# Gated linear attention and a ReLU-squared layer on one core: where three of twelve units transpose the attention's output

## The chip, the core and the metric

The kernel runs on one core of a Trainium2 chip. A core has five engines with a program each: TensorE (PE in the profile; PEld is its weight load), VectorE (DVE), ScalarE (ACT), GpSimd (POOL) and SyncE (SP), which here only issues DMAs. The metric is the time of one execution on the chip in microseconds (us), median of several runs. Lower is better.

## What is computed

A recurrent attention with decays, then a dense layer with a squared ReLU:

```python
for t in range(S):                                   # S = 768, B = 4, H = 8, D = 48
    state = alpha[:, :, t, :, None] * state + np.einsum('bhd,bhe->bhde', k[:, :, t], v[:, :, t])
    y[:, :, t] = np.einsum('bhd,bhde->bhe', q[:, :, t], state)
x = y.transpose(0, 2, 1, 3).reshape(B * S, H * D)    # 3072 x 384
h = x @ w_in                                         # 384 x 2048
r = np.maximum(h, 0.0)
out = (r * r) @ w_out                                # 2048 x 384
```

Inputs and output are float32; the kernel multiplies in bfloat16 and accumulates in float32.

## The kernel before

The work is cut into 12 **units**, each 256 tokens of one of the four sequences; unit g is batch g % 4, step g // 4. The names below are those of the kernel's operations; `_g` is the unit.

1. **Loads.** `lda`, `ldk`, `ldq`, `ldv` bring alpha, k, q and v of a unit (384 KB each, L540). Units 0 to 3 come in part over POOL's queue with the weights `win0` to `win2` and `wout0`, `wout1` (L508), all else over SP's queue.
2. **Decays.** `pr` multiplies the decays of two neighbouring tokens (L656 on VectorE, L658 on POOL), `ln` takes the logarithm, `m1i` sums it along tokens on TensorE (L668), `ei`, `ea`, `es` are exponentials on ScalarE, `bk` and `aq` products (L686, L697).
3. **Scaled keys and queries.** `ekm` and `eqm` multiply them by k and q (L737, L732). From unit 3 on, two DMA transposes per unit, `tr0` and `tr1`, turn them over on SP's queue (L748); before that TensorE does it.
4. **Scores.** `p0_g` multiplies keys and queries into the four banks psX and psZ (L926), `mk0` and `mk1` mask them into SBUF on VectorE (L937).
5. **State and output.** `vc` casts v to bfloat16 (L727 on POOL, L728 on ScalarE). `y_g` multiplies masked scores and state with v into psX (L818, L829); in its middle it also makes the state product of unit g+1 (`kv`, L797), so it waits for `vc_(g+1)`. `sa`, `sc`, `sd` update the state (L892 to L903).
6. **Transposing the output.** `xe_g` copies psX to bfloat16 (xbf, L957). Then either SP issues one DMA transpose `xt_g` from xbf to xt (L978), or TensorE makes six transposes of 128 x 128 into psX (L972) and `xv_g` copies them to xt (L984). The set `DMA_X` says which: units 4 to 11 go over SP's queue, units 0 to 3 over TensorE.
7. **First layer.** `s1_g_u`, u from 0 to 7, six matmuls of 256 columns each (L1030); `re` is the ReLU (L1038 on ScalarE, L1040 on VectorE), `sq` the square.
8. **Second layer.** For units 3 to 10 a Strassen form with seven products in two halves each (`s2_g_m10` to `s2_g_m71`, four matmuls of 192 columns, L1096) and sums of operands before (`ga`, `gb`, `gc`; `ws` for the weights) and of results behind (`ca` to `cg`, L1123 to L1127). Units 0 to 2 and 11 use plain products of 384 columns (L1168, L998). `out` stores the unit over SP's queue. The output tile osb has two buffers, so the first write of unit g waits for the store of unit g-2.

The order of every engine is written out by hand in `ORDERS`: one list of names per engine, and an operation may be in the list of one engine or of another where it has both forms. A planner only works out which waits are needed; it changes no order. Each engine takes its list strictly from the front, so one operation that waits holds all behind it. That holds for SP's queue too, where a transpose, a load or a store that waits for its source holds the later DMAs. A few loads are tied to the landing of an earlier one (`AFTER`: `win2` before `wout0`, for example). Fillers, `fill512` and `fill256`, are products with zeros that keep TensorE busy while it waits at the start.

Of the kernel before, what the change touches and what calls it, by code (L numbers as in the profile page):

```python
# [1263 lines left out]
```

## Time and profile before

| | us |
|---|---|
| median of 3 runs | 174.56 (174.54 to 178.17) |
| profiled execution | 176.19 |
| its span, first to last instruction | 174.5 |
| TensorE busy | 161.7 |
| VectorE busy | 136.1 |
| ScalarE busy | 122.5 |
| GpSimd busy | 100.0 |

The profile is of one execution. A line of a timeline gives the start, the length, the engine, the line of the kernel and the operation, and in brackets how long the engine sat idle ahead of it and what ended that. A matmul's end is modelled, and matmuls overlap, so the pace of TensorE is read from one start to the next. "SPq" is a DMA being issued on SP's queue, not its transfer. The granted clock of TensorE was 1.000 of full speed.

### The profile page before, as it was taken

The page shows a single profiled execution, that of the slowest core. Times are in us where ns is not written, and L with a number is a line of the kernel's source. Part 1 is how long each engine was busy: PE and PEld are TensorE (multiplying, and loading weights), DVE is VectorE, ACT ScalarE, POOL GpSimd, SP SyncE. Part 2 cuts the span into 40 slices and gives each one's busy share as a digit, 9 for nine tenths or more (in the row PEclk, how much of TensorE's full clock was granted, in tenths as well). Part 3 has the DMA queues.
Part 4 walks back from the last instruction along what each step waited for, and adds up shares of the span by engine and source line. Part 5 has one row for each costly group of instructions (what it writes and reads, how often), then busy time and mean ns, then how long its engine had stood idle before and what let it go on. Part 6 is the DMA issues. An engine that isn't in the chain of part 4 may idle for free.

```text
span 174.5 us, 5592 instructions
## 1 busy us (share of the span) xinstructions
PE 161.7 (93%) x2417; PEld 139.2 (80%) x2417; DVE 136.1 (78%) x230; ACT 122.5 (70%) x213; POOL 100.0 (57%) x95
## 2 busy tenths in 40 slices
PE   7789989999999799899977989899899999999994
PEld 2456879757788587799966879799889999999973
DVE  4588889998898798789868797869999559855620
ACT  4775579968979499698887568798866775576310
POOL 3935263910188467696724864789854780938140
PEclk9999999999999999999999999999999999999999
DMA  5999999997899998999999998999787770400122
GB/s 141 332 306 210 298 258 218 250 328 159 164 215 181 340 238 167 292 157 243 288 137 229 292 143 195 155 228 316 121 144 235 75 184 4 135 4 19 71 94 92
DMA packets 70633, 33.40 MB, mean 191 GB/s; under 512 B 66544, under 2 KB 67568, under 8 KB 70608
## 3 DMA queue, kind: packets, MB, share of 16 engines
q1 hardware_dynamic: 67984, 26.35, 69.6%
q0 software_dynamic: 2624, 6.69, 15.7%
q8 instruction: 19, 0.31, 0.7%
q14 instruction: 6, 0.05, 0.1%
HBM read 25.17 MB, written 4.72 MB: 171 GB/s over the span
## 4 chain that ended last, share of the span: by engine, by line
PE 43%; DMA 23%; DVE 15%; SPq 8%; POOL 4%; issue 3%; ACT 2%; DVEq 0%; ACTq 0%
PE psWH L1030 16%; DMA out_dram<-osb 8%; PE psO L1096 7%; DMA raw<-in_alpha_dram 6%; PE psWH L1096 5%; SPq L540 5%; DMA win<-in_moe_w_in_dram 5%; PE psO L1168 5%; DVE pm L937 4%; DMA raw<-in_k_dram 3%; DMA raw<-in_v_dram 2%; DVE prd L656 2%; DVE rr L1040 2%; POOL raw L540 2%; SPq L748 2%
## 5 line engine op out<-in xcount | busy, mean ns | idle before, releaser
L1030 PE MATMUL psWH<-xt,win 128*128 128x256 bf16 x552 | 71.5, 273 | 0.4 <-DMA win<-in_moe_w_in_dram 0.4
L1030 PEld LDWEIGHTS psWH<-xt,win 128*128 128x128 bf16 x552 | 60.1, 129 | 2.1 <-DMA win<-in_moe_w_in_dram 0.6
L1038 ACT ACTIVATE rr<-psWH 128x512 bf16<-128x512 f32 x69 | 40.2, 594 | 14.8 <-PE psWH L1030 13.9
L1052 ACT ACTIVATE gt<-rr 128x1024 bf16<-128x1024 bf16 (+1 forms) x40 | 37.2, 946 | 2.7 <-DVE rr L1040 2.5
L1082 POOL TENSOR_TENSOR gt<-sg,gt 128x512 bf16<-128x512 bf16 x15 | 18.6, 1237 | 14.9 <-DVE sg L1080 14.8
L1051 POOL TENSOR_TENSOR gt<-rr 128x512 bf16<-128x512 bf16 (+1 forms) x12 | 14.7, 1228 | 15.5 <-ACT rr L1038 13.2
L1040 DVE TENSOR_SCALAR rr<-psWH 128x512 bf16<-128x512 f32 x23 | 15.8, 685 | 5.2 <-PE psWH L1030 5.1
L1168 PE MATMUL psO<-wout,gt 128*128 128x384 bf16 x96 | 18.3, 326 | 0.0
L937 DVE TENSOR_TENSOR pm<-psZ,caus 128x1024 bf16<-128x1024 f32 x12 | 14.6, 1218 | 2.4 <-PE psZ L926 2.4
L937 DVE TENSOR_TENSOR pm<-psX,caus 128x1024 bf16<-128x1024 f32 x12 | 14.6, 1217 | 1.5 <-PE psZ L926 1.5
L1096 PE MATMUL psWH<-sw,gt 128*128 128x192 bf16 x128 | 15.1, 246 | 0.0
L1096 PE MATMUL psO<-wout,gt 128*128 128x192 bf16 x128 | 13.7, 246 | 1.3 <-ACT osb L1123 0.7
L1083 POOL TENSOR_TENSOR sh<-gt 128x512 bf16<-128x512 bf16 x10 | 13.4, 1341 | 2.2 <-DVE gt L1082 1.3
L1080 DVE TENSOR_TENSOR sg<-gt 128x1024 bf16<-128x1024 bf16 x13 | 12.5, 961 | 1.9 <-PE psWH L1096 1.0
L732 DVE TENSOR_TENSOR qks<-raw,eq 128x384 bf16<-128x384 f32 x18 | 12.6, 712 | 1.5 <-DMA raw<-in_q_dram 1.4
L727 POOL CAST vbf<-raw 128x768 bf16<-128x768 f32 x8 | 7.8, 978 | 10.1 <-DMA raw<-in_v_dram 10.0
L1168 PEld LDWEIGHTS psO<-wout,gt 128*128 128x128 bf16 x96 | 8.9, 98 | 4.7
L957 ACT ACTIVATE xbf<-psX 128x768 bf16<-128x768 f32 x11 | 8.9, 807 | 5.0 <-PE psX L818 3.3
L1096 PEld LDWEIGHTS psO<-wout,gt 128*128 128x128 bf16 x128 | 10.5, 98 | 2.0 <-ACT osb L1123 1.0
L737 DVE TENSOR_TENSOR qks<-raw,ek 128x768 bf16<-128x768 f32 x11 | 10.4, 946 | 2.0 <-DMA raw<-in_k_dram 1.8
L1096 PEld LDWEIGHTS psWH<-sw,gt 128*128 128x128 bf16 x128 | 10.6, 98 | 0.6
L1127 DVE TENSOR_TENSOR osb<-psWH,osb 128x192 f32<-128x192 f32 x24 | 8.4, 351 | 3.1 <-PE psWH L1096 3.0
(162 smaller groups left out, 297.5 us busy)
## 6 DMA issues: line engine op xcount, KB each, us to landing
out_dram<-osb SPq DMA_DIRECT2D x11, 384.0 KB, 5.1
raw<-in_alpha_dram SPq DMA_DIRECT2D x10, 384.0 KB, 4.8
raw<-in_q_dram SPq DMA_DIRECT2D x10, 384.0 KB, 5.4
raw<-in_v_dram SPq DMA_DIRECT2D x10, 384.0 KB, 4.6
raw<-in_k_dram SPq DMA_DIRECT2D x9, 384.0 KB, 5.1
wout<-in_moe_w_out_dram POOLq DMA_DIRECT2D x2, 768.0 KB, 8.0
raw<-in_k_dram POOLq DMA_DIRECT2D x3, 384.0 KB, 6.4
raw<-in_alpha_dram POOLq DMA_DIRECT2D x2, 384.0 KB, 6.3
```

The source lines that it names most:

```text
L732: add("dve", lambda e, j=j, dst=dst: e.tensor_tensor(dst, RAW[r][:, 2, :, j, :].rearrange("p (n x) d -> p n x d", x=2), EQ[la][:, j].rearr ...
L937: add("dve", lambda e, hf=hf, psT=psT: e.tensor_tensor(PM[pm][:, hf].rearrange("p r n j t -> p (r n) (j t)"), psT[:, :, :].rearrange("p r ...
L1030: ins = pe.matmul(psF[:, i * T:(i + 1) * T], WIN[:, kk, hidden(fj)], mov, start=(kk == 0), stop=(kk == KT - 1))
L1038: add("act", lambda e, psF=psF, rr=rr: e.activation(rr, psF, AF.Relu), act_ns(512), pu + 600, reads=[keyF], writes=[("rr", rb, half)], nam ...
L1040: alts={"dve": (lambda e, psF=psF, rr=rr: e.tensor_scalar(rr, psF, 0.0, None, ALU.max), dve_ns(512))})
L1051: alts={"pool": (lambda e, dst=dst, sq=sq: e.tensor_tensor(dst, sq, sq, ALU.mult), 200 + k * 840), "act": (lambda e, dst=dst, sq=sq: e.act ...
L1052: "act": (lambda e, dst=dst, sq=sq: e.activation(dst, sq, AF.Square), act_ns(k * 512))})
L1080: ga = lambda e, us=us: e.tensor_tensor(SG[:, us], view(us, 128, [[0, 2], [1, 128]]), view(us, 0, [[384, 2], [1, 128]]), ALU.subtract)
L1082: gb = lambda e, us=us: e.tensor_tensor(G4[:, us, 0, 1], SG[:, us, 1], G4[:, us, 0, 0], ALU.subtract)
L1083: gc = lambda e, us=us: e.tensor_tensor(SH[:, us], G4[:, us, 1, 0], G4[:, us, 0, 1], ALU.add)
L1096: ins = pe.matmul(psS, left(u), right(u), start=(first and u == 0), stop=(u == nu - 1), skip_group_check=True)
L1168: ins = pe.matmul(psS, GT[gt][:, fj, j, :], WOUT[:, fj, :], start=(fj == 0), stop=(fj == FT - 1))
```

## The change

Units 4, 6 and 8 leave `DMA_X`: their `xt` is six transposes on TensorE into psX, with a copy `xv` on VectorE. SP's list has three names fewer. All five lists are new, and many operations change places, and some their engine.

```diff
-    DMA_X = (4, 5, 6, 7, 8, 9, 10, 11)
+    DMA_X = (5, 7, 9, 10, 11)
```

SP's list:

```diff
-        lda0 ldk0 ldq0 ldv0 ldv1 lda3 ldq3 lda4 ldk4 ldq4 tr0_3 tr1_3 ldv4 lda5 ldq5 tr1_4 tr0_4 ldk5 lda6 ldv5 ldk6
-        out0_1 ldq6 out1_1 tr1_5 tr0_5 xt4 ldv6 lda7 ldq7 ldk7 tr1_6 tr0_6 xt5 ldv7 lda8 ldk8 ldq8 out2_1 tr1_7 tr0_7
-        xt6 ldv8 lda9 ldq9 ldv9 ldk9 out3_1 tr0_8 tr1_8 xt7 lda10 out4_1 tr1_9 tr0_9 ldq10 ldk10 xt8 ldv10 lda11
...
+        lda0 ldk0 ldq0 ldv0 ldv1 lda3 ldq3 lda4 ldq4 ldk4 tr0_3 tr1_3 lda5 ldv4 ldq5 ldk5 tr1_4 tr0_4 ldv5 lda6 lda7
+        out0_1 ldq6 tr1_5 tr0_5 ldk6 ldv6 out1_1 ldk7 ldq7 tr1_6 tr0_6 xt5 ldv7 lda8 ldq8 ldk8 out2_1 tr0_7 tr1_7 ldv8
+        lda9 ldk9 tr1_8 tr0_8 ldq9 out3_1 xt7 ldv9 lda10 ldk10 ldq10 out4_1 tr1_9 tr0_9 ldv10 lda11 ldq11 out5_1 ldv11
...
```

TensorE's list at the start, and around the three transposes and unit 4's scores:

```diff
...
-        fill512_15 fill512_16 fill256_17 fill256_18 y0 tr1_1 fill512_19 fill256_20 xt0 tr0_1 fill512_21 fill512_22
-        fill512_23 fill256_24 p0_1 s1_0_0 s1_0_2 s1_0_1 kv1 s1_0_3 y1 s1_0_4 s1_0_6 xt1 s1_0_5 m1i2 s1_0_7 s1_1_0 m1s2
...
-        s1_2_3 s1_2_2 p0_3 s2_1_1_0 s2_1_1_1 s1_2_4 s1_2_5 y3 s2_1_1_2 s1_2_7 m1i5 xt3 s1_2_6 s2_1_1_3 s1_3_1 s1_3_0
-        p0_4 s2_2_0_0 s2_2_0_1 s1_3_3 s2_2_0_2 s1_3_2 y4 s2_2_0_3 s1_3_5 m1i6 s1_3_4 s2_2_1_0 s1_3_7 s2_2_1_1 s1_3_6
...
+        fill512_15 fill256_16 fill256_17 tr0_1 xt0 tr1_1 fill256_18 s1_0_2 p0_1 s1_0_0 s1_0_1 kv1 s1_0_3 y1 s1_0_4
+        s1_0_5 xt1 s1_0_7 m1i2 s1_0_6 m1s2 s1_1_2 s1_1_1 s1_1_0 s1_1_5 s1_1_4 tr0_2 s1_1_3 tr1_2 s1_1_7 s2_0_0_0 p0_2
...
+        xt3 m1i5 s1_2_6 s2_1_1_3 s1_3_1 s1_3_0 s2_2_0_0 p0_4 s2_2_0_1 s1_3_3 s1_3_2 s2_2_0_2 y4 s1_3_5 s2_2_0_3 m1i6
+        s1_3_4 s1_3_7 s2_2_1_0 xt4 s2_2_1_1 s2_2_1_2 s2_2_1_3 s1_3_6 p0_5 s2_3_m10 s1_4_0 s1_4_1 s2_3_m60 s2_3_m11
...
+        s2_3_m51 s1_5_0 s1_5_1 s2_3_m40 s2_3_m30 s1_5_2 s2_3_m31 s1_5_3 y6 s2_3_m41 s1_5_4 s2_4_m10 xt6 s2_4_m11 m1i8
+        s1_5_5 s2_4_m20 s2_4_m60 s2_4_m21 s1_5_6 s2_4_m61 s1_5_7 s2_4_m50 s2_4_m70 p0_7 s2_4_m71 s2_4_m51 s1_6_0
...
+        s2_5_m40 s1_7_3 s2_5_m41 s1_7_4 m1i10 xt8 s2_5_m30 s2_5_m31 s2_6_m60 s1_7_5 s1_7_6 s2_6_m10 s2_6_m61 s2_6_m11
+        s1_7_7 s2_6_m20 p0_9 s2_6_m21 s1_8_0 s2_6_m70 s2_6_m71 s1_8_1 s2_6_m50 s2_6_m51 s1_8_2 y9 s2_6_m40 s1_8_3
...
```

POOL's list at the start, and VectorE's lines with the three new copies and with sa10:

```diff
-        #20 #22 #14 #21 #15 lda1 ldq1 ldk1 win1 vc0 win0 win2 lda2 ldv2 ldk2 ldq2 wout0 sd1 sd0 wout1 sq1_1 ldv3 ldk3
...
+        #14 #21 #20 #15 #22 lda1 ldk1 ldq1 win1 vc0 win0 win2 lda2 ldk2 vc1 ldv2 ldq2 sd0 wout0 pr2 wout1 sd1 bk2 aq2
...
```

```diff
-        mk1_8 cd5 ce5 re7_2 sa9 re7_3 ga6_1 cf5 cg5 lb10 eqm1_10 ca6 cb6 ekm10 mk0_9 mk1_9 cd6 eqm0_10 ce6 pr11 xe9
-        sa10 ga7_1 cf6 cg6 sq8_1 re8_6 lb11 ca7 gc7_1 re8_7 mk1_10 cb7 mk0_10 ekm11 cd7 eqm1_11 eqm0_11 ga8_0 gc7_0
...
+        oe2_0 ga3_0 gb3_0 sc5 re3_7 lb6 gc3_0 xv4 eqm0_6 eqm1_6 ekm6 mk0_5 mk1_5 ga3_1 gb3_1 re4_3 sa6 cb3 sc6 cc3
+        re4_4 eqm1_7 cd3 lb7 ekm7 ga4_0 ce3 mk1_6 mk0_6 eqm0_7 pr8 sq4_5 cg3 sa7 cf3 sc7 xv6 gc4_0 gb4_1 lb8 cc4
...
+        ekm9 eqm0_9 mk0_8 cd5 eqm1_9 re7_2 gc5_0 sa9 cf5 ce5 ga6_1 re7_4 xv8 cg5 re7_5 eqm1_10 lb10 ekm10 cb6 mk0_9
+        mk1_9 eqm0_10 cd6 re8_1 ce6 sa10 xe9 ga7_1 cg6 cf6 lb11 eqm1_11 sq8_6 mk1_10 cb7 mk0_10 ekm11 eqm0_11 cd7 ce7
...
```

In the new lists `pr11` is POOL's, and so are `pr2`, `bk2`, `aq2` and `bk3`; `vc3`, `vc4`, `vc5`, `vc7` and `vc9` go to ScalarE. TensorE has 11 fillers of 512 columns in place of 17.

More of the change, by code (lines that the diff above doesn't have):

```diff
@@ L25 @@
+        sq9_5 re9_7 cc8 re10_1 sq9_7 re10_3 xe11 re10_5 re10_4 re10_7 re10_6 sq10_1 sq10_5 re11_1 cc9 re11_3 re11_2
+        re11_5 sq11_1 sq11_3 ca10 cc10 sq11_5 oe11_10
     """,
     "dve": """
-        #19 #5 #3 #1 #12 #10 #9 #11 #13 #8 #7 #16 ekm0_0 eqm0_0 ekm1_0 et10_0 #17 et01_0 #18 #6 eqm1_0 sa0 mk0_0 mk1_0
-        eqm1 #2 ekm1 et1_1 et0_1 sc0 mk1_1 mk0_1 sa1 sc1 re0_3 re0_2 pr2 xv1 sq0_3 bk2 ekm2 re1_0 aq2 eqm2 #4 et0_2
-        et1_2 sq0_7 ws0_0 sq1_5 mk1_2 mk0_2 pr3 ws0_1 sa2 sc2 bk3 ekm3 aq3 eqm1_3 eqm0_3 pr4 sd2 sq1_6 xv2 ws3_0 sc3
@@ L70 @@
-        sd7 gc6_0 sq7_7 sq7_6 ga7_0 gb7_0 gb7_1 vc11 sq8_7 bk11 gb8_0 ga8_1 gb8_1 gc8_0 sq9_7 gb9_0 gc9_0 gb9_1 gc9_1
-        gb10_0 sq10_7 gc10_0 gb10_1 sq11_7 sq11_6
+        #14 #21 #20 #15 #22 lda1 ldk1 ldq1 win1 vc0 win0 win2 lda2 ldk2 vc1 ldv2 ldq2 sd0 wout0 pr2 wout1 sd1 bk2 aq2
+        vc2 sq1_1 ldk3 ldv3 ws0_1 bk3 bk4 sd3 pr5 ws3_0 ws2_1 ws3_1 bk5 sq2_7 sq2_5 pr6 sq3_3 bk6 pr7 sq3_6 vc6 gc3_1
+        ws1_1 sd5 bk7 gb4_0 sq4_6 ga4_1 bk8 sq5_7 vc8 gc4_1 pr9 gb5_0 gb5_1 gc5_1 sq6_6 sd6 ga6_0 pr10 gb6_0 gb6_1
```

78 lines of the change are left out of this document (35 added, 43 removed).

## The prediction

> **What bounds the kernel now.** I read the engine sums first, then the same sums cut into stretches, then the waits of TensorE alone, then the order of time on SP's queue around each wait.
>
> ```profile
> span 174.5 us, 5592 instructions
> PE 161.7 (93%) x2417; PEld 139.2 (80%) x2417; DVE 136.1 (78%) x230; ACT 122.5 (70%) x213; POOL 100.0 (57%) x95
> ```
>
> TensorE (PE) is the busiest engine, 174.5 - 161.7 = 12.8 us idle. The next view is the table of stretches: length, busy time of PE, weight loads, VectorE (DVE), ScalarE (ACT), GpSimd (POOL), then PE's clock, DMA share, GB/s.
>
> ```profile
> 0.00:17.73 17.73, 14.24 (x211) 8.39 (x212) 12.05 (x31) 10.67 (x19) 10.36 (x20) 1.00 1.00 247
> 17.73:60.00 42.27, 41.26 (x580) 32.91 (x580) 36.67 (x55) 32.80 (x61) 19.87 (x18) 1.00 1.02 237
> 60.00:100.00 40.00, 36.09 (x632) 32.51 (x632) 33.98 (x54) 32.65 (x58) 26.80 (x24) 1.00 1.08 230
> 100.00:130.00 30.00, 28.11 (x424) 26.02 (x422) 26.39 (x42) 23.99 (x42) 21.97 (x17) 1.00 1.01 188
> 130.00:172.20 42.20, 42.01 (x572) 39.36 (x572) 26.76 (x53) 22.42 (x37) 21.00 (x17) 1.00 0.37 93
> ```
>
> Before 17.73 us PE waits for the first weights and is partly fed with fillers. From there to 172.20 it is bound by its own work, with idle time of 1.01 + 3.91 + 1.89 + 0.19 = 7.0 us, 5.8 of it from 60 to 130 us, where the DMA share is about 1. From 130 on nothing but PE counts. So the time is: arrival of the weights, plus PE's work, plus these stalls, plus a tail. The timeline of PE names the long stalls (start, length, [idle before <- who ended it]):
>
> ```profile
> 61.14 0.19 PE L818 MATMUL psX<-sbd,kqt 64*128 64x48 bf16 x1 [1.32 <-DVE pm L937]
> 72.85 0.19 PE L818 MATMUL psX<-sbd,kqt 64*128 64x48 bf16 x1 [0.68 <-POOL vbf L727]
> 96.09 0.19 PE L818 MATMUL psX<-sbd,kqt 64*128 64x48 bf16 x1 [1.16 <-POOL vbf L727]
> 103.99 0.83 PE L1096 MATMUL psO<-wout,gt 128*128 128x192 bf16 x8 [0.74 <-ACT osb L1123]
> 113.02 0.34 PE L668 MATMUL psZ<-lab,linc 128*128 128x384 bf16 x1 [0.45 <-ACT lab L659]
> 126.69 0.32 PE L668 MATMUL psZ<-lab,linc 128*128 128x384 bf16 x1 [0.66 <-DVE smd L892]
> ```
>
> These are, in order, y4, y5, y7, the second layer of unit 5, m1i10 and m1i11. SP's queue shows what lay behind four of them:
>
> ```profile
> 47.10 5.46 SPq L748 DMA_TRANSPOSE kqt<-qks  x2
> 52.61 1.47 SPq L540 DMA_DIRECT2D raw<-in_k_dram  x1
> 65.48 1.86 SPq L978 DMA_TRANSPOSE xt<-xbf  x1
> 67.39 0.58 SPq L540 DMA_DIRECT2D raw<-in_v_dram  x1
> 88.46 2.28 SPq L978 DMA_TRANSPOSE xt<-xbf  x1
> 90.79 0.58 SPq L540 DMA_DIRECT2D raw<-in_v_dram  x1
> 96.40 1.15 SPq L1145 DMA_DIRECT2D out_dram<-osb  x1
> 97.59 5.99 SPq L748 DMA_TRANSPOSE kqt<-qks  x2
> 103.63 1.29 SPq L978 DMA_TRANSPOSE xt<-xbf  x1
> 104.96 0.58 SPq L540 DMA_DIRECT2D raw<-in_alpha_dram  x1
> ```
>
> Here v6 is issued at 67.39, right behind xt4, and v8 at 90.79, right behind xt6; the casts that y5 and y7 wait for follow as they land. k5 is issued at 52.61, behind both halves of tr_4, and holds up ekm5, which stands ahead of unit 4's masks on VectorE; y4 waits for those masks. a10 is issued at 104.96 behind xt7 and ends in the wait of m1i10.
>
> **The change part by part.** *Added on TensorE and VectorE.* xt4, xt6 and xt8 become six transposes and one copy each. The chain of waits and the groups by form give their price today:
>
> ```profile
> 42.12 0.33 PE psX L972 x6
> L984 DVE COPY xt<-psX 128x768 bf16<-128x768 bf16 x3 | 1.7, 553 | 0.4 <-PE psX L972 0.2
> ```
>
> The next piece of PE starts at 42.46, so PE pays 3 x 0.34 = **+1.0 us**, fully on the path, since PE is what sets the end. VectorE gets 3 x 0.55 = 1.7 us, beside 136.1 of 174.5; it costs nothing while the copy lands before the next scores. *The new wait:* xt_g waits for xe_g (the evacuation of psX on ScalarE), and the scores p of the next unit wait for xv_g, because all share psX. What stands between y_g and xt_g on PE hides the first: for unit 4 five steps and more, for unit 6 s2, s1, s2, for unit 8 s2, s1, s2, s1, m1i. The prices of these, and unit 7's end of y and xe:
>
> ```profile
> 69.38 1.47 PE L1030 MATMUL psWH<-xt,win 128*128 128x256 bf16 x12
> 70.69 0.82 PE L1096 MATMUL psO<-wout,gt 128*128 128x192 bf16 x8
> 71.35 0.82 PE L1030 MATMUL psWH<-xt,win 128*128 128x256 bf16 x6
> 97.14 0.50 PE L1096 MATMUL psWH<-sw,gt 128*128 128x192 bf16 x4
> 97.25 0.81 ACT L957 ACTIVATE xbf<-psX 128x768 bf16<-128x768 f32 x1 [2.57 <-PE psX L818]
> ```
>
> Twelve L1030 matmuls take 70.69 - 69.38 = 1.31 us, so an s1 step of six is 0.66; eight L1096 take 71.35 - 70.69 = 0.66, so an s2 step of four is 0.33. PE goes on from y7 at 97.14, and xe7 ends at 98.06, so an xt could start 1.0 us after y. Unit 6 has 1.3 us of cover for that and unit 8 about 2.1. Behind each xt stand at least 2.6 us before the next scores, against 0.34 and 0.55 for xt and its copy, and what is ahead of that on VectorE. I cost the wait at nothing; without the cover it is rival C.
>
> *Removed from SP's queue.* Three issues go: 1.86 and 2.28 us for xt4 and xt6 in the rows above, and xt8, with no long stall of PE behind it:
>
> ```profile
> 113.42 2.87 SPq L978 DMA_TRANSPOSE xt<-xbf  x1
> ```
>
>  What follows in the queue moves up by as much: v8, now right behind tr_7, by 2.3 us against a stall of 1.16, and v6 by 1.86 less the issue of k6, which now stands ahead of it (as long as k5's at most, 1.47), so 0.4, and by another 1.3 as tr_5, whose sources VectorE makes behind unit 4's masks, comes earlier with y4. I count 0.68 + 1.16 = **-1.8 us**.
>
> *Moved on SP's queue.* ldk5 now stands ahead of tr_4: k5 is issued at about 47.1, 5.5 us earlier, and y4's stall goes, **-1.3**. The price is that tr_4 is issued one load (1.47 us) later. p0_4 waits for it; one s2 step of 0.65 was put ahead of p0_4, so I count 0.75 back. lda10 no longer stands behind all of unit 7's late queue: **-0.45**. out3 moves behind tr_8 (5.99 us in the row) and a load; ca5 already waited for it (stall 0.74). With xt6 gone and four loads behind, not ahead of, tr_8, it is issued 1 to 2 us later: I count 1.0 back.
>
> *Moved between engines.* pr11 goes to POOL, and sa10 ahead of xe9, on which m1i11 waited: **-0.66**. By the lists, VectorE goes from 230 to 237 instructions, ScalarE from 213 to 212 and POOL from 91 to 88; none comes near PE's 161.7 us.
>
> *The start.* Six fillers of 512 columns go (17 to 11), and s1_0_2, which reads only win1, comes ahead of p0_1 and of s1_0_0, which waits for win0:
>
> ```profile
> 14.96 0.93 POOL L540 DMA_DIRECT2D raw<-in_alpha_dram  x1 [4.50 <-DMA win<-in_moe_w_in_dram]
> 17.73 0.84 PE L1030 MATMUL psWH<-xt,win 128*128 128x256 bf16 x6 [0.43 <-DMA win<-in_moe_w_in_dram]
> ```
>
> The load of a2 is held by win1, so win1 is there by 14.96; win0 by 17.73. One s1 step leaves the time after 17.73: **-0.66**. Bounds: 0 if xt0's copy comes too late, -0.66 as only one step reads win1 alone here.
>
> *Unknown.* The rest of the new order has no rows. Its stalls lie between 0 and 7.0 us, what the old order has in all. Of the old 7.0 I have named 4.27 that go; the other 2.7 I leave. For stalls that are new I take 1.0 beside the 1.75 above, nearest to the many small ones (0.4 to 0.7) of the old order.
>
> Sum: 1.02 - 1.84 - 1.32 - 0.45 - 0.66 - 0.66 + 1.75 + 1.0 = **-1.2 us**. The profiled execution took 176.19 us, 1.7 more than its span, the median of the runs is 174.56; I carry the difference over: **173.4 us**.
>
> How much DMA time a transpose takes decides whether the loads also land faster. Two stretches of 2 us, one of loads and a store, one of tr_5 and xt4:
>
> ```profile
> 60.00:62.00 2.00, 0.86 (x58) 0.87 (x60) 2.00 (x2) 2.00 (x4) 1.91 (x3) 1.00 1.07 348
> 64.00:66.00 2.00, 2.00 (x18) 1.70 (x17) 2.00 (x5) 1.94 (x6) 0.69 (x1) 1.00 0.98 75
> ```
>
> At an equal share of the DMA engines, 348 GB/s are moved there and 75 here. An xt of 128 x 768 x 2 bytes = 197 KB is then 2.6 us of all engines, and three are 7.9 us of a stretch of 70 that is full. I take nothing for this beyond the terms above. [...]
>
> **The rivals.** *B, the relief is swallowed:* loads are late for other reasons (the DMA share is 1.0 from 0 to 130 us whatever is queued), the stalls of 4.27 come back elsewhere. Then only the start and the transposes count: -0.66 + 1.02 = +0.4, **174.9 us**. For it: the named stalls have five different causes, and the new lists reorder every engine, so each pair of neighbours that caused none may cause one now. Against: two of the stalls stand directly behind an xt that is gone. That the change does not do what it says (the gain comes from ldk5 and pr11, not from the transposes) would show as an unchanged y5 and y7; its time lies between B and the forecast.
>
> *C, slower, the new ring on psX:* xe_g stands behind ln_(g+2) on ScalarE, and that waits for the product pr on POOL or VectorE.
>
> ```profile
> ACT lab L659 <- POOL prd L658: 4.9, 4, 2.3
> PEld psX L972 <- ACT xbf L957: 0.2, 1, 0.2
> ```
>
> With a wait of 2.3 us there (the longest), xt6 is late by 2.3 + 1.0 - 1.3 = 2.0 us and xt8 by 2.3 + 1.0 - 2.1 = 1.2; PE stands still, and everything behind it. On top of B: 174.9 + 3.2 = **178.1 us**. It decides once ln comes over 0.3 us (unit 6) or 1.1 us (unit 8) after the end of y. Against it: units 0 to 3 run this chain now, with one wait of 0.2 us (the second row).
>
> *D, clean:* the named stalls go and nothing new comes: 1.02 - 4.27 - 0.66 = -3.9, **170.6 us**.
>
> **How the numbers follow.** Forecast 0.45, B 0.30, C 0.15, D 0.10. About 2% (3.5 us) is what a measurement of this kernel can tell from no change. Faster by more, under 171.1: D and a little of the forecast's lower end, 0.11. Slower by more, over 178.1: half of C and the edge of B with the unknown stalls, 0.10. Within: 0.79. The range leaves out about half of D and half of C: 170.8 to 177.4.
>
> **What would show it.** L972 has 42 matmuls, and SP issues five xt. y4 and y7 start without a wait over 0.3 us; the first s1 starts before 17 us; the stretch from 60 to 130 has under 4 us of idle PE. A wait of PE on L957 (xbf), or of the scores on L984, shows C. If PE's idle time after 17.73 is again 7 us but under other names, it is B. The prediction is wrong if the front (17.73 to 60 us, now 1.0 us idle) gets stalls of its own: pr2, bk2 and aq2 now stand on POOL behind the issue of wout, and such a product takes 1.02 us there in place of 0.55:
>
> ```profile
> L688 DVE TENSOR_TENSOR ek<-ek,raw 128x384 f32<-128x384 f32 x3 | 1.7, 553 | 0.9 <-ACT ek L679 0.9
> L686 POOL TENSOR_TENSOR ek<-ek,raw 128x384 f32<-128x384 f32 x7 | 7.1, 1020 | 6.4 <-ACT ek L679 6.3
> ```

## The result and the profile after

The changed kernel takes **0.989 of the time before, 95% interval 0.9855 to 0.9929**: 174.56 x 0.9892 = 172.7 us, 1.9 us less (1.2 to 2.5). The forecast was 1.2 us less, 173.4 us. Six of the 20 executions after the change and 14 of the 20 before enter this comparison, those up to 1.5% above the fastest of their kernel; 13 of the 14 left out after the change show a granted clock of 0.98 or 0.99, no trace of any of them was kept, and over all executions the plain medians tie (175.07 us after, 175.03 before).

The profiled execution took 172.51 us (176.19 before, which is 1.6 us over the median before, so the two profiles lie further apart than the times). In this kernel the line numbers are two lower than in the one before: L1028 is the first layer, L1094 the second, L816 and L827 y, L970 the transposes on TensorE, L982 their copy, L935 the masks. The experiments below are numbered like the kernel before, except where said. First the engine sums of the page of the kernel after:

```profile
span 170.8 us, 5611 instructions
PE 161.3 (94%) x2429; PEld 139.0 (81%) x2429; DVE 137.1 (80%) x237; ACT 121.6 (71%) x212; POOL 101.9 (60%) x92
```

The stretches of the kernel after (length, then busy time of PE, weight loads, DVE, ACT, POOL, then PE's clock, DMA share, GB/s):

```profile
15.94:60.00 44.06, 41.66 (x606) 32.48 (x607) 38.30 (x54) 31.41 (x57) 29.97 (x27) 1.00 1.01 234
60.00:100.00 40.00, 39.27 (x667) 35.25 (x666) 36.70 (x62) 33.39 (x61) 23.84 (x21) 1.00 1.06 225
100.00:130.00 30.00, 30.00 (x483) 28.49 (x482) 27.42 (x44) 25.73 (x45) 26.05 (x21) 1.00 0.95 218
130.00:168.50 38.50, 38.33 (x508) 35.71 (x505) 23.09 (x52) 20.63 (x33) 13.52 (x9) 1.00 0.30 72
```

From the first s1 step to the end of PE's work, idle time went from 7.0 to 2.40 + 0.73 + 0 + 0.17 = 3.3 us. The first s1 starts 1.79 us earlier (15.94 against 17.73 us), but PE's work from there on is 149.26 against 147.47 us: 1.0 us of it are the new transposes, the rest is what used to stand ahead of 17.73. So of the 3.7 us between the two spans, all is idle time, and it went from 60 to 130 us (5.80 to 0.73); the front got worse (1.01 to 2.40).

PE's stalls in the timeline of the kernel after, all of those over 0.3 us from the first s1 on:

```profile
17.85 1.50 PE L1028 MATMUL psWH<-xt,win 128*128 128x256 bf16 x12 [0.49 <-DMA win<-in_moe_w_in_dram]
41.07 0.36 PE L856 MATMUL psX<-smd,kqt 128*64 128x96 bf16 x8 [0.78 <-ACT vbf L726]
51.40 0.19 PE L816 MATMUL psX<-smd,kqt 64*128 64x48 bf16 x1 [0.34 <-ACT vbf L726]
73.96 0.19 PE L816 MATMUL psX<-sbd,kqt 64*128 64x48 bf16 x1 [0.73 <-DVE pm L935]
```

These are the first s1 on win0, then y2, y3 and y5. y4, y7, m1i10 and m1i11 no longer wait. y5 does, but for another engine: its v is there, its masks (`pm`, L935) are late. SP's queue of the kernel after:

```profile
47.62 1.64 SPq L538 DMA_DIRECT2D raw<-in_k_dram  x1
49.31 4.97 SPq L746 DMA_TRANSPOSE kqt<-qks  x2
...
61.22 4.53 SPq L746 DMA_TRANSPOSE kqt<-qks  x2
65.80 0.58 SPq L538 DMA_DIRECT2D raw<-in_k_dram  x1
66.42 0.58 SPq L538 DMA_DIRECT2D raw<-in_v_dram  x1
...
87.97 1.01 SPq L538 DMA_DIRECT2D raw<-in_v_dram  x1
```

k5 now goes out at 47.62, ahead of tr_4; v8 at 87.97, 2.8 us earlier than before. But k6 is issued at 65.80, behind both halves of tr_5: the new order does to unit 6 what the old one did to unit 5, and y5 pays 0.73 us for it. One transposition set costs PE what was expected (chain of waits, kernel after; the next step starts at 87.65):

```profile
87.32 0.33 PE psX L970 x6
```

### The profile page after: what moved, and what is told of

The parts are those of the page before. It is cut to its first block, busy times and chain, and to the rows that moved or that the text cites. A ratio compares the mean times of both kernels' runs of the same rounds, so it can differ in the third digit from the quotient of the medians.

```text
span 170.8 us, 5611 instructions
## 1 busy us (share of the span) xinstructions
PE 161.3 (94%) x2429; PEld 139.0 (81%) x2429; DVE 137.1 (80%) x237; ACT 121.6 (71%) x212; POOL 101.9 (60%) x92
## 4 chain that ended last, share of the span: by engine, by line
PE 65%; DMA 14%; DVE 9%; SPq 4%; POOL 4%; issue 1%; ACT 1%; DVEq 0%
PE psWH L1028 26%; PE psO L1094 12%; PE psWH L1094 10%; DMA raw<-in_alpha_dram 4%; PE psO L1166 4%; DMA win<-in_moe_w_in_dram 4%; SPq L746 3%; DVE pm L935 3%; DMA raw<-in_v_dram 3%; DMA raw<-in_k_dram 2%; DVE qks L735 2%; PE psX L827 2%; PE psZ L795 2%; POOL raw L538 2%; PE psX L924 2%; PE psX L996 2%
## 5 line engine op out<-in xcount | busy, mean ns | idle before, releaser
L1028 PE MATMUL psWH<-xt,win 128*128 128x256 bf16 x552 | 72.3, 273 | 0.8 <-DMA win<-in_moe_w_in_dram 0.8
L1028 PEld LDWEIGHTS psWH<-xt,win 128*128 128x128 bf16 x552 | 59.9, 129 | 2.8 <-ACT rr L1036 1.0
L1036 ACT ACTIVATE rr<-psWH 128x512 bf16<-128x512 f32 x67 | 39.0, 595 | 16.6 <-PE psWH L1028 15.9
L1050 ACT ACTIVATE gt<-rr 128x1024 bf16<-128x1024 bf16 (+1 forms) x38 | 35.4, 952 | 0.5 <-DVE rr L1038 0.3
L1049 POOL TENSOR_TENSOR gt<-rr 128x512 bf16<-128x512 bf16 (+1 forms) x13 | 19.2, 1489 | 7.5 <-ACT rr L1036 5.7
L1078 POOL TENSOR_TENSOR sg<-gt 128x1024 bf16<-128x1024 bf16 x5 | 11.1, 2211 | 15.9 <-PE psWH L1094 11.2
L1038 DVE TENSOR_SCALAR rr<-psWH 128x512 bf16<-128x512 f32 x25 | 17.1, 685 | 1.9 <-PE psWH L1028 1.5
L684 POOL TENSOR_TENSOR ek<-ek,raw 128x384 f32<-128x384 f32 x9 | 10.1, 1118 | 9.7 <-ACT ek L677 9.7
L935 DVE TENSOR_TENSOR pm<-psZ,caus 128x1024 bf16<-128x1024 f32 x12 | 14.6, 1218 | 0.7 <-PE psZ L924 0.7
L1094 PE MATMUL psWH<-sw,gt 128*128 128x192 bf16 x128 | 15.0, 246 | 0.0
L1094 PE MATMUL psO<-wout,gt 128*128 128x192 bf16 x128 | 15.0, 246 | 0.0
L1080 POOL TENSOR_TENSOR gt<-sg,gt 128x512 bf16<-128x512 bf16 x9 | 11.4, 1266 | 5.7 <-DVE sg L1078 5.5
L935 DVE TENSOR_TENSOR pm<-psX,caus 128x1024 bf16<-128x1024 f32 x12 | 14.6, 1216 | 0.1
L735 DVE TENSOR_TENSOR qks<-raw,ek 128x768 bf16<-128x768 f32 x11 | 13.2, 1197 | 1.8 <-DMA raw<-in_k_dram 0.7
L1081 POOL TENSOR_TENSOR sh<-gt 128x512 bf16<-128x512 bf16 x9 | 10.5, 1181 | 2.9 <-DVE gt L1080 2.7
L1094 PEld LDWEIGHTS psO<-wout,gt 128*128 128x128 bf16 x128 | 10.8, 98 | 0.5
L1094 PEld LDWEIGHTS psWH<-sw,gt 128*128 128x128 bf16 x128 | 10.8, 98 | 0.4
```

Of the source, the lines that this page charges most:

```text
L735: add("dve", lambda e, a=a, E=E: e.tensor_tensor(QKS[qs][:, a, :, :, 0:D], RAW[r][:, 1 + a].rearrange("p h j d -> p j h d"), E[la][:].rear ...
L935: add("dve", lambda e, hf=hf, psT=psT: e.tensor_tensor(PM[pm][:, hf].rearrange("p r n j t -> p (r n) (j t)"), psT[:, :, :].rearrange("p r ...
L1028: ins = pe.matmul(psF[:, i * T:(i + 1) * T], WIN[:, kk, hidden(fj)], mov, start=(kk == 0), stop=(kk == KT - 1))
L1036: add("act", lambda e, psF=psF, rr=rr: e.activation(rr, psF, AF.Relu), act_ns(512), pu + 600, reads=[keyF], writes=[("rr", rb, half)], nam ...
L1038: alts={"dve": (lambda e, psF=psF, rr=rr: e.tensor_scalar(rr, psF, 0.0, None, ALU.max), dve_ns(512))})
L1049: alts={"pool": (lambda e, dst=dst, sq=sq: e.tensor_tensor(dst, sq, sq, ALU.mult), 200 + k * 840), "act": (lambda e, dst=dst, sq=sq: e.act ...
```

## Experiments

**Theory:** the gain comes from the three DMA transposes that are gone; the new order of the lists gives little. **Rival:** the gain is the order's (k5, pr11, the start), and the transposes by themselves are worth 0.8 us or less. The two halves of the change are tried apart first.

### Old lists, only the transposes moved (e2)

```diff
-    DMA_X = (4, 5, 6, 7, 8, 9, 10, 11)
+    DMA_X = (5, 7, 9, 10, 11)
  SP:      xt4, xt6, xt8 out of the old list
  TensorE: ... s2_2_1_0 [xt4] ... s1_5_4 [xt6] ... m1i10 [xt8] ...
  VectorE: ... lb6 [xv4] ... ca4 [xv6] ... re7_3 [xv8] ...
```

> The old lists, with xt4, xt6 and xt8 on TensorE and their copies on VectorE, nothing else. Queue theory: the stalls of y5 (0.68) and y7 (1.16) shrink under 0.3, 42 transposes cost 1.0 more than 24, so 0.8 us faster than before. Order theory: the stalls stay or move, 0.5 to 1.0 us slower than before. The stall of y4 (1.32) stays by both.

Measured: ratio **0.989 (0.983 to 0.995)**, as good as the whole change; the medians over all executions, 171.99 against 173.74 us, give 0.990. Its stretches and its two longest stalls:

```profile
60.00:100.00 40.00, 38.70 (x669) 35.28 (x667) 36.83 (x61) 34.58 (x61) 27.77 (x27) 1.00 1.10 248
100.00:130.00 30.00, 30.00 (x481) 28.48 (x479) 27.16 (x44) 23.79 (x42) 22.96 (x18) 1.00 0.81 188
```

```profile
39.94 0.36 PE L858 MATMUL psX<-smd,kqt 128*64 128x96 bf16 x8 [0.92 <-DVE qks L737]
61.53 0.19 PE L818 MATMUL psX<-sbd,kqt 64*128 64x48 bf16 x1 [1.29 <-DVE pm L937]
```

y4 waits as before (k5 has not moved). y5 and y7 do not wait any more, as forecast, but neither do the second layer of unit 5, m1i10 and m1i11, whose ends I had credited to other edits or not at all. y2's wait is new: before, none there was over 0.3 us.

### New lists, the transposes put back on SP's queue (e1, e5)

```diff
-    DMA_X = (5, 7, 9, 10, 11)
+    DMA_X = (4, 5, 6, 7, 8, 9, 10, 11)
-        out0_1 ldq6 tr1_5 tr0_5 ldk6 ...  out2_1 tr0_7 tr1_7 ldv8 ...  ldk10 ldq10 out4_1 tr1_9 tr0_9 ldv10 ...
+        out0_1 ldq6 tr1_5 tr0_5 xt4 ldk6 ...  out2_1 tr0_7 tr1_7 xt6 ldv8 ...
   e1:   ldk10 ldq10 xt8 out4_1 tr1_9 tr0_9 ldv10 ...
   e5:   ldk10 ldq10 out4_1 tr1_9 tr0_9 xt8 ldv10 ...
```

> The new lists of every engine, but xt4, xt6 and xt8 go back to SP's queue (behind tr_5, tr_7 and ldq10), off TensorE and VectorE. Queue theory (v6 and v8 came late because an xt stood ahead of them): y5 and y7 wait for vbf again by 0.7 to 1.2 us each, TensorE has 1.0 us less, so 0.2 to 0.9 us slower than the changed kernel. Order theory (the time came from moves that do not hang on xt: k5, pr11, the start): no new stall, 1.0 us faster than the changed kernel.

> As the first run (the new lists, xt4, xt6 and xt8 back on SP's queue), but with xt8 behind tr_9, where the old list has it; in the first run it stood ahead of tr_9 and p0_9 waited 1.4 us for that. If the first run's 2% came from that place, this is within 0.5% of the kernel before. If the new lists cannot bear the three transposes on SP at all, it is again 1.5 to 2% slower than before.

Measured: e1 1.0192 (1.0139 to 1.0244), e5 **0.9985 (0.9923 to 1.0047)**. e1 says little about the question, because I put xt8 ahead of out4 and tr_9, which it then held up: PE stands still twice, for 1.61 and 1.43 us, around 117 us. e5, with xt8 behind both, is the fair one. With it the two halves make a table of four ratios:

| | transposes on SP's queue | units 4, 6, 8 on TensorE |
|---|---|---|
| old lists | 1 | 0.989 (e2) |
| new lists | 0.9985 (e5) | 0.989 (the change) |

Taking the transposes off SP gives 1.1% in the first row and 0.9% in the second. Changing the lists gives 0.15% in one column and nothing in the other, both inside the intervals. By the ratios the theory holds and the rival falls.

The waits expected of e1 and e5 did not come back, though. In both profiles y7 has none, and y5 waits for its masks (1.63 and 0.76 us), not for v. So by which waits the new lists lose their 0.9% is not shown. The longest stall of e5's profile stands elsewhere, behind a product of VectorE (L732) that took 2.48 us beside one of POOL, and the clock falls to 0.50 after it (last section):

```profile
134.95 0.82 PE L1096 MATMUL psO<-wout,sh 128*128 128x192 bf16 x4 [1.94 <-DVE osb L1127]
```

That execution took 176.8 us, and e5's median is 176.1 us.

### Two edits of the lists alone, on the kernel before (e3, e4)

```diff
  e3, SP:
-        lda0 ldk0 ldq0 ldv0 ldv1 lda3 ldq3 lda4 ldk4 ldq4 tr0_3 tr1_3 ldv4 lda5 ldq5 tr1_4 tr0_4 ldk5 lda6 ldv5 ldk6
+        lda0 ldk0 ldq0 ldv0 ldv1 lda3 ldq3 lda4 ldk4 ldq4 tr0_3 tr1_3 ldv4 lda5 ldq5 ldk5 tr1_4 tr0_4 lda6 ldv5 ldk6
  e4, TensorE:
-        ... fill512_21 fill512_22 fill512_23 fill256_24 p0_1 s1_0_0 s1_0_2 s1_0_1 ...
+        ... fill256_24 s1_0_2 p0_1 s1_0_0 s1_0_1 ...
```

> The old kernel with one move on SP's queue: ldk5 ahead of tr_4. Order theory: the stall of y4 (1.32 us) goes, p0_4 waits up to 0.75 us for tr_4, so 0.6 to 1.3 us faster than before. Rival: the stall only moves from y4 to p0_4, no change.

> The old kernel with s1_0_2 ahead of p0_1 and three fillers fewer. Order theory: the first s1 starts near 16.4 in place of 17.73 us, one s1 step (0.66 us) leaves the time after win0's landing, 0.66 us faster than before if nothing later eats it. Rival: the front is bound by a chain of unit 1 and 2 (pr2, ln2, m1i2), the gain turns into a longer wait at m1i2 and no time is gained.

Measured: e3 0.9951 (0.9904 to 0.9999), e4 0.9989 (0.9948 to 1.003). In e3, y4's stall is gone, and p0_4 ahead of it has one as long. I had allowed 0.75 us there, as tr_4 is issued later. The profile puts this one down to "issue", nothing that it shows, but the rows of tr_4 (durations of the two issues, their starts, then the times to landing) account for it:

```profile
57.06 0.42 PE L926 MATMUL psX<-kqt 64*64 64x128 bf16 x16 [1.50 <-issue]
```

```profile
L748 SPq DMA_TRANSPOSE kqt<-qks x2: 1315/2480/3646, 48.3 to 51.9; - x2
DMA to landing us min/median/max: 5.0/5.4/5.9
```

The second half of tr_4 is issued at 51.9 us and lands 5.0 us later at the earliest, at 56.9, right ahead of p0_4 at 57.06. Before, it was issued at 51.3 and took 4.0 us (p0_4 at 55.81, no wait). So with k5's load ahead of it that half is issued 0.6 us later and takes 1.0 us longer to land. The stretch behind, in the same execution, has no idle time at all, though xt4 and xt6 are on SP's queue; with the later start of what follows, y5 and y7 can be on time so too:

```profile
60.00:100.00 40.00, 40.00 (x676) 36.67 (x675) 35.55 (x59) 35.14 (x62) 28.25 (x26) 1.00 1.13 245
```

That execution took 171.2 us, the shortest of e3's, whose median is 173.6 us, so it is not how e3 mostly runs.

In e4 the first s1 starts at 16.25 us in place of 17.73, and then PE waits for the logarithm of unit 2:

```profile
16.25 0.84 PE L1030 MATMUL psO<-xt,win 128*128 128x256 bf16 x6 [0.35 <-ACT xt L986]
...
24.41 0.34 PE L668 MATMUL psWH<-lab,linc 128*128 128x384 bf16 x1 [0.49 <-ACT lab L659]
```

k5's edit is worth 0.9 us (0 to 1.7) where 1.32 - 0.75 = 0.6 was forecast; the start's 0.2 us (0.9 faster to 0.5 slower) where 0.66 was. Both forecasts lie in their intervals, and these runs don't decide more than that.

### Unread transfers in place of the transposes that went (e6, e7)

Is it SP's queue, in which a transpose holds up what stands behind it, or the DMA engines, which it keeps busy? e2 gets back three transfers of 192 KB from xbf to a tile that nobody reads, at the places of xt4, xt6 and xt8: DMA transposes in e6, plain copies in e7. Lines from the transfers on are one (up to L978) to six higher.

```diff
+    if g in (4, 6, 8):
+        add("sp", lambda e: e.dma_start_transpose(tg, src), ... reads=[("xbf", x2)], writes=[("xg",)], name=f"xtg{g}")   # e6
+        add("sp", lambda e: e.dma_start(tg, src), ... reads=[("xbf", x2)], writes=[("xg",)], name=f"xtg{g}")             # e7
```

> The old lists with xt4, xt6 and xt8 on TensorE, and three DMA transposes of the same sources into a buffer that nobody reads, where SP's list had the three xt. All of TensorE's extra work is paid and none of SP's relief is had. Queue theory: the stalls of y5 and y7 come back, 0.0 to 0.6% slower than before. If the gain has another source (xt ready earlier, so s1 and the evacuations are better placed), it stays 1% faster than before.

> As the run with the three unread DMA transposes, but plain copies of the same 197 KB in their place. If the place in SP's queue is what costs (a command more, the wait for xbf), this is as slow as with the unread transposes. If the time of the transposes on the DMA engines costs (2.6 us each at 75 GB/s against 0.6 at 348), it is nearly as fast as without any: 0.7 to 1.1% faster than before.

Measured: e6 **1.0024 (0.9974 to 1.0073)**, e7 **0.9936 (0.9882 to 0.999)**, against 0.989 for e2. The transposes take all of the gain back, 1.3%; copies of the same bytes in the same places about 0.5%, though e7's interval touches both neighbours: e6's begins 0.0016 below its end (the medians over all executions are 176.3 us for e6 and 174.9 us for e7). In e6's profile y7 waits for v again, and so does y6, which did not before; y5 does not, and m1i10 waits 0.70 us (that execution took 178.0 us):

```profile
85.35 0.18 PE L819 MATMUL psX<-sbd,kqt 64*128 64x48 bf16 x1 [1.09 <-POOL vbf L728]
96.34 0.19 PE L819 MATMUL psX<-sbd,kqt 64*128 64x48 bf16 x1 [1.09 <-POOL vbf L728]
```

e7 has no stall at y5, y6, y7 or m1i10. Both have a longer one than before at m1i11 (1.46 and 1.47 us, see below), more than the 0.8 us that e7 loses against e2. What the queue holds is similar (issues of 1.83, 1.29 and 1.74 us in e6, of 1.44, 1.15 and 2.33 us in e7), so the place in the queue is not the whole of it. The pages give the DMA engines' time on SP's queue as a share of the span; here are the lines of e6 and e7 in this order (packets, MB, share):

```profile
q1 hardware_dynamic: 67984, 26.35, 67.4%
```

```profile
q1 hardware_dynamic: 66016, 26.35, 66.8%
```

Times the spans (176.3 and 173.0 us here), the pages of all kernels with eight, five, or five and three copies give:

| transfers from xbf on SP's queue | kernels | us of all 16 engines | mean |
|---|---|---|---|
| 8 transposes | before, e1, e3, e4, e5, e6 | 121.5, 119.2, 117.2, 118.6, 117.3, 118.8 | 118.8 |
| 5 transposes | after, e2, e8, e11, e12 | 114.4, 111.8, 113.4, 114.7, 112.5 | 113.4 |
| 5 transposes, 3 copies | e7 | 115.6 | 115.6 |

That is (118.8 - 113.4) / 3 = 1.8 us of all 16 engines for each transpose, less than the 2.6 us that the prediction read from one row. Kernels that move the same lie up to 4.3 us apart, so the 1.8 is rough. The three copies are 115.6 - 113.4 = 2.2 us together, 0.7 each, less than the spread. By these means a transpose took more of the engines than a copy of the same bytes, 1.8 against 0.7 us, with that spread.

### Which of the three counts, and how far it goes (e8, e9, e10)

e8 is e2 with the loads of k5 and q5 exchanged around tr_4; e9 is e8 with xt8 back on SP's queue; e10 is e8 with xt5 and xt7 on TensorE too.

```diff
  e8, SP (from e2):
-        ... ldv4 lda5 ldq5 tr1_4 tr0_4 ldk5 lda6 ldv5 ...
+        ... ldv4 lda5 ldk5 tr1_4 tr0_4 ldq5 lda6 ldv5 ...
  e8, VectorE:
-        ... xv3 eqm1_5 lb5 ... mk0_4 mk1_4 eqm0_5 ...
+        ... xv3 lb5 ... mk0_4 mk1_4 eqm1_5 eqm0_5 ...
  e9 (from e8):  DMA_X = (5, 7, 8, 9, 10, 11);  SP: ... ldq10 ldk10 xt8 ldv10 ...
  e10 (from e8): DMA_X = (9, 10, 11);  TensorE: ... m1i7 xt5 ... m1i9 xt7 ...;  VectorE: ... re4_4 xv5 ... cg4 xv7 ...
```

> The old lists with xt4, xt6 and xt8 on TensorE, and ldk5 and ldq5 exchanged around tr_4, with eqm1_5 behind unit 4's masks on VectorE. The stall of y4 (1.29 in the run with xt alone) goes and p0_4 gets none, as tr_4 is issued no later. If stalls add up: 0.7% faster than with xt alone, 1.8% than before. If the stall only moves to the next late load: as fast as with xt alone.

> The old lists with the fifth unit's key load ahead of its q load, and only units 4 and 6 transposed on TensorE; unit 8 goes through SP's queue as before. It stands against the run with all three on TensorE (ratio 0.985). The prediction's own term gave the removal of unit 8's DMA transpose no gain and 0.34 us of TensorE for it: by that this kernel is 0.2% faster than the one with three (ratio 0.983), and no stall comes back between 100 and 130 us. The rival, that a DMA transpose slows the other transfers in flight wherever it stands: the 0.7 and 0.66 us stalls at m1i10 and m1i11 come back, the DMA's share between 100 and 130 us rises from about 0.81 towards 0.95, and the kernel is 0.3 to 0.8% slower than the one with three (ratio 0.988 to 0.993).

> As the kernel with three units on TensorE and the earlier key load, with units 5 and 7 on TensorE too, right behind their m1i7 and m1i9. Two more sets of six transposes cost 2 x 0.34 = 0.67 us of TensorE and two copies on VectorE of about 0.4 us each. If the gain was that of stalls which are gone by now (about 1.9 us of idle TensorE are left behind 16 us, most of it not due to SP's queue), this one is 0.4% slower than the kernel with three (ratio 0.989). If the DMA engines' relief still pays, it is equal or faster (0.980 to 0.985), with the DMA's share between 60 and 100 us below that of the kernel with three.

Measured: e8 **0.9853 (0.9782 to 0.9924)**, e9 0.9868 (0.9816 to 0.9919), e10 0.9949 (0.991 to 0.9987). e8 is the fastest seen, though not told apart from the changed kernel, from e2 or from e9. e10 is slower than e8 by about 1%, with intervals that just touch: the two further sets, 0.67 us of PE, find nothing left to pay for them (their copies took 0.55 us each, not 0.4).

e9 brings back m1i11's stall of 0.66 us, to the hundredth that of before. m1i10 does not wait, and the DMA share from 100 to 130 us is 0.89, against 0.82 in e8; e9's interval holds the prediction's 0.983 and much of the rival's range, so the ratio decides nothing. The timelines of VectorE, POOL and PE around it show what it hangs on. Before:

```profile
122.67 2.12 POOL L1080 TENSOR_TENSOR sg<-gt 128x1024 bf16<-128x1024 bf16 x1 [0.33 <-ACT gt L1052]
122.94 2.27 DVE L656 TENSOR_TENSOR prd<-raw 128x384 f32<-128x384 f32 x1
```

e8, where nothing waits:

```profile
118.82 2.45 POOL L1080 TENSOR_TENSOR sg<-gt 128x1024 bf16<-128x1024 bf16 x1
118.34 0.93 DVE L656 TENSOR_TENSOR prd<-raw 128x384 f32<-128x384 f32 x1
```

e9:

```profile
121.18 2.13 POOL L1080 TENSOR_TENSOR sg<-gt 128x1024 bf16<-128x1024 bf16 x1 [0.55 <-ACT gt L1052]
121.24 2.49 DVE L656 TENSOR_TENSOR prd<-raw 128x384 f32<-128x384 f32 x1
125.20 0.32 PE L668 MATMUL psZ<-lab,linc 128*128 128x384 bf16 x1 [0.66 <-DVE smd L892]
```

L656 is pr11. When POOL's product sg has started just before it, pr11 does not end until sg has (before: 122.67 + 2.12 = 124.79, and pr11 at 125.21), and the state update smd behind it on VectorE, for which m1i11 waits, is late. When pr11 starts first, it takes 0.93 us: in e8 it started beside POOL's product before sg (L1051, which ended at 118.85), ended 0.42 us after that, and sg was the one held, 2.45 us in place of 2.12. The ten profiled executions in which pr11 is VectorE's fall into three groups:

| kernels | pr11's start less sg's, us | pr11 takes, us | stall at m1i11, us |
|---|---|---|---|
| e2, e8, e10, e12 | -0.48 to -0.47 | 0.92 to 0.94 | none |
| before, e3, e4, e9 | 0.06 to 0.28 | 2.26 to 2.49 | 0.66 |
| e6, e7 | 2.74 | 1.24 | 1.46, 1.47 |

In these profiles, then, the removal of xt8 is worth m1i11's 0.66 us by putting pr11 half a microsecond ahead of a product on another engine, and all four in which xt8 is gone and no unread transfer stands in its place have it so. What moves pr11 against sg I have not varied by itself. (e9's execution took 174.7 us, its median is 172.6 us; before, e3 and e4 show the same 0.66.)

### The new lists mended, and a further step from e8 (e11, e12)

```diff
  e11 (the changed kernel), POOL and SP:
-        ... ldk3 ldv3 ...          lda5 ldv4 ldq5 ldk5 ...      ldq6 tr1_5 tr0_5 ldk6 ldv6 ...
+        ... ldv3 ldk3 ...          ldv4 lda5 ldq5 ldk5 ...      ldq6 ldk6 tr1_5 tr0_5 ldv6 ...
  e12 (e8), SP and POOL:
-        ... tr1_4 tr0_4 ldq5 lda6 ldv5 ldk6 ...      ... pr6 vc5 ...
+        ... tr1_4 tr0_4 ldv5 lda6 ldq5 ldk6 ...      ... vc5 pr6 ...
```

> The changed kernel with three loads put back ahead of what its new lists set before them: the third unit's v load ahead of its key load on POOL's queue, the fourth's ahead of lda5 and the sixth's key load ahead of tr1_5 on SP's. In the changed kernel y2, y3 and y5 wait 0.78, 0.34 and 0.73 us for these. If stalls add up, 1.85 us go, which is 1.0% (ratio 0.978 to the kernel before). If what hides behind them is as late (as in the run in which the k5 load alone was moved, where 1.06 us went and 1.50 us came at p0_4), it stays at the changed kernel's ratio of 0.989.

> The kernel with three units on TensorE and the earlier key load, with the fifth unit's v load right behind tr0_4, its q load behind lda6, and its v copy ahead of pr6 on POOL: y4's remaining wait of 0.91 us is for that v. If it goes without an heir the kernel is 0.5% faster than the one it starts from (ratio 0.980); if the q load, now later, is what p0_5 or m1i6 waits for, it is equal (0.985).

Measured: e11 1.0031 (0.9986 to 1.0076), e12 0.9942 (0.9902 to 0.9983). Both miss: each removes the waits that it aims at and loses more elsewhere. In e12, y4 starts without a wait worth the name, and then:

```profile
60.98 1.95 POOL L1060 TENSOR_TENSOR sw<-wout 128x768 bf16<-128x768 bf16 x1
```

```profile
60.38 2.96 DVE L732 TENSOR_TENSOR qks<-raw,eq 128x384 bf16<-128x384 f32 x2 [1.21 <-DMA raw<-in_q_dram]
```

```profile
64.01 0.88 PE L1030 MATMUL psWH<-xt,win 128*128 128x256 bf16 x6 [2.07 <-DVE rr L1040]
```

Two products of 0.55 us each (the q load now lands later) meet POOL's sw, which ends at 62.93, end only after it, at 63.34, and the ReLU behind them on VectorE is late: 0.91 us saved, 2.07 paid. For e11, the profile shows y3's and y5's waits gone and others in their place, such as this one for a product on POOL:

```profile
61.97 0.83 PE L1168 MATMUL psO<-wout,gt 128*128 128x384 bf16 x4 [1.90 <-POOL gt L1051]
```

The longest of e11's profile is at y11:

```profile
131.90 2.12 POOL L1080 TENSOR_TENSOR sg<-gt 128x1024 bf16<-128x1024 bf16 x1 [1.08 <-PE psO L1096]
```

```profile
132.13 2.71 DVE L737 TENSOR_TENSOR qks<-raw,ek 128x768 bf16<-128x768 f32 x1 [1.36 <-DMA raw<-in_k_dram]
```

```profile
134.89 0.19 PE L818 MATMUL psX<-sbd,kqt 64*128 64x48 bf16 x1 [2.09 <-DVE qks L737]
```

ekm11 starts 0.23 us after POOL's sg and takes 2.71 us. In the profile of the changed kernel, with the same lists here, it starts 0.87 us ahead of sg (129.51 against 130.38 us) and takes 0.96. That execution of e11 took 177.9 us, and its median is 176.6 us, so why its ratio is a whole 1.4% above that of the kernel it starts from is left open.

## Why the prediction was right, and where it was not

**The size and the place.** The forecast of -1.2 us stands against -1.9 (-2.5 to -1.2): within 2%, on the fast side, inside the range. The range also holds B's 174.9 us and no change at all, so lying in it says little. TensorE's 1.0 us for the transposes and the copy's 0.55 us came as worked out; the stalls that went lay between 60 and 130 us, as the stretches said they must. Of its signs, those on y4, y7, the first s1 and the stretch from 60 to 130 us came true.

**The transposes** were summed as +1.02 - 1.84 = -0.8 us. Alone they bring -1.9 (e2, -0.9 to -3.0). The step that failed is "I take nothing for this beyond the terms above" behind the DMA time, with xt8's removal set at nothing: beside y5 and y7, the stalls of unit 5's second layer (0.74), m1i10 (0.45) and m1i11 (0.66) went with them. By the stalls, 0.68 + 1.16 + 0.74 + 0.45 + 0.66 - 1.02 is 2.7 us; 1.9 was measured. (Two more, of 0.52 and 0.41 us near 90 us, went as well, and y2 got one of 0.92.) The row of 75 GB/s had a reason in it, and e6 and e7 (1.0024 and 0.9936) show that what a transpose takes beyond a copy counts; with transposes y7 and m1i10 wait in e6's profile, with copies in e7's they do not. Unit 5's second layer waits in neither, so its 0.74 is not explained, and m1i11's 0.66 hangs on which of two products starts first.

**The order of the lists** was summed as -1.32 - 0.45 - 0.66 - 0.66 + 1.75 + 1.0 = -0.3 us and is worth 0 to -0.3 (the table of four). That sum is right by balance, which is luck, and not by its terms. k5's earlier load hands its stall on to p0_4 in e3's profile (1.32 us gone, 1.50 new). lda10 and pr11 take the credit for stalls that go without them (e2). The first s1 starts 1.8 us earlier in the changed kernel and 1.5 in e4, and e4 gains no time that could be told from none. The prediction named a worse front as a sign that it is wrong, and on the front it was: idle time there rose by 1.4 us, but not through pr2, bk2 and aq2 as it supposed: y2 and y3 wait for the casts of v3 and v4, whose loads the new lists put behind others. out3, counted at 1.0 us late, holds up nothing.

**The rivals.** B, that the relief is swallowed, fails: its 174.9 us lies outside the interval (172.0 to 173.3), and in the profiles idle time fell from 7.0 to 3.3 us. It is right about the lists, whose gains were swallowed one by one. D, the clean case, fails too: y2, y3 and y5 wait anew, and 170.6 us lies outside the interval. C, the ring on psX, did not happen: these are the waits for the transposes and their copies, of who waited for whom in the kernel after (total, times, longest):

```profile
DVE xt L982 <- PE psX L970: 1.5, 3, 0.7
PEld psO L1028 <- DVE xt L982: 0.3, 1, 0.3
PEld psX L924 <- DVE xt L982: 0.2, 1, 0.2
```

VectorE waits for the transposes, PE never for xbf, and the scores (L924) once for a copy, 0.2 us, where C supposed 2.0 and 1.2. "The gain comes from ldk5 and pr11, not from the transposes" is the reverse of what the runs show.

## What to carry to other kernels

When the DMA engines are at full share (1.08 and 1.01 before, from 60 to 130 us), count what a transfer takes of them and not only its issue: a transpose of 192 KB took, by an estimate from the table of e6 and e7, about 1.8 us of all of them, and 0.34 us on TensorE with a copy of 0.55 us on VectorE. An edit of the order that aims at one stall is seldom worth that stall's length (e3, e11 and e12 each had a new one elsewhere, of the same size or longer), so try a set of edits together and each half alone before crediting it. Before placing a product on VectorE whose operands are both in SBUF, see which instruction of GpSimd it can meet: in the profiles here 68 of 68 ended only 0.41 to 0.57 us after it (below). Half a microsecond of order decided between 0 and 0.66 us, and stalls of 1.94, 2.09 and 2.07 us (e5, e11, e12) stood behind such meetings.

## What the runs showed of the hardware

**VectorE held by GpSimd.** In the profiled executions of before, e2, e3, e8, e11 and e12 together, 68 products of VectorE with both operands in SBUF started beside a running POOL instruction (31 of L1080, 28 of L732, 9 of L656, counted where the timeline has the instruction in a row of its own). Every one of them ended a fixed time after that instruction: 0.53 to 0.57 us for L1080, 0.41 to 0.43 us for L732 and L656. So 20, 16 and 8 of them took over 0.25 us longer than the shortest of their kind. Those with an operand in PSUM never did (L892, L899, L937: 0 of 162, 21 of which started beside no more than the issue of a DMA on POOL). Where VectorE's pr11 started first, POOL's product took longer: sg 2.45 us in e8 (118.82 us) in place of 2.12 before (122.67 us).

**One order, different stalls.** e8 and e10 have the same lists up to y4, and in their timelines (e8 first) y4 waits 0.91 and 1.61 us for the same cast, at 60.72 and 62.10 us:

```profile
60.72 0.18 PE L818 MATMUL psX<-sbd,kqt 64*128 64x48 bf16 x1 [0.91 <-POOL vbf L727]
```

```profile
62.10 0.18 PE L818 MATMUL psX<-sbd,kqt 64*128 64x48 bf16 x1 [1.61 <-POOL vbf L727]
```

In e9, which again is the same up to there, the wait is 1.86 us. A stall read from one profiled execution is therefore uncertain by up to about 1 us, as much as most terms of the sum.

**A stall that can cost twice.** In e1, two stalls within 4 us left PE idle for more than half of the time, and then the granted clock fell to half for over 3 us (stretches of 1 us; the clock is the third number from the end):

```profile
118.00:119.00 1.00, 0.00 (x0) 0.01 (x1) 0.00 (x0) 0.95 (x2) 1.00 (x2) 0.85 0.48 77
119.00:120.00 1.00, 0.98 (x32) 0.85 (x32) 0.00 (x0) 0.00 (x0) 1.00 (x2) 0.50 1.02 267
120.00:121.00 1.00, 1.00 (x10) 0.89 (x7) 0.86 (x1) 0.12 (x1) 0.74 (x1) 0.50 1.16 321
121.00:122.00 1.00, 1.00 (x7) 0.69 (x6) 1.00 (x2) 0.21 (x1) 0.00 (x0) 0.50 1.17 323
122.00:123.00 1.00, 1.00 (x12) 0.99 (x11) 0.49 (x1) 0.84 (x2) 0.71 (x1) 0.94 1.14 357
```

By the clock column that is, as an estimate, 0.15 + 3 x 0.50 + 0.06 = 1.7 us lost on top of the 3.0 of the stalls. The same came behind one stall: after the 1.94 us of e5 (134.95 us) and the 2.09 us of e11 (134.89 us) the clock fell to half as well, and the same sum gives 1.7 us for each; the mean granted clock of the executions of e1, e5 and e11 is 0.99. In e5:

```profile
135.00:136.00 1.00, 1.00 (x7) 0.84 (x8) 1.00 (x4) 0.00 (x0) 0.00 (x0) 0.50 0.54 86
```

It need not: the stalls of 2.07 us in e12 (64.01 us) and of 1.90 us in e11 (61.97 us) left the clock at 1.00. What decides between the two these runs do not show.
